# Output matmuls one batch behind instead of two, w_out loaded ahead of batch 1, packed-times-w_in in single two-bank PSUM tiles

## The chip, the cores and the metric

The kernel runs on one core of one Trainium2 chip. The metric is the device time of one execution in microseconds (us), median of several executions. An execution over 1.5% longer than the fastest of its kernel would count as slow.

## The reference

Eight batches of 576 tokens go through two attentions with 32 packed rows a head, then through a layer of width 2048 with `h * cos(h)`:

```python
p_packed = sm_attn(p, k, v)                 # 8 batches x 8 heads, 32 packed rows, head_dim 64
out = sm_attn(q, p_packed, p_packed)        # 576 queries a batch
x = out.transpose(0, 2, 1, 3).reshape(4608, 512)
h = x @ w_in                                # w_in 512 x 2048
g = h * cos(h)
return g @ w_out                            # w_out 2048 x 512, float32 out
```

## The kernel before

It never forms `x`. For each batch it computes PPW = packed rows times w_in (in the code `ppw`), and then the hidden layer as PPW times the normalised second-attention weights (`h_mm`, one call for each of 16 column blocks of 128, "layers" here). A batch goes through: key transpose, first scores and exp (`s1`), transposed probabilities (`a1T`), first product (`pp`), `ppw`, query transpose, second scores and exp (`s2`), sums and normalisation, 16 times `h_mm` with cos on ScalarE and the gate product on VectorE, and at last the output matmuls, 64 of 128x512 for an even batch and 80 for an odd one (`out_gen`). The order of instructions on each engine is the order of the program. The output matmuls are the "filler": `fill(n)` puts n of them between the steps of a later batch.

PSUM is the memory that matmuls write to. A tile in it comes free when ScalarE or VectorE has read it for the last time; reading it out to SBUF, the chip's other memory, is called evicting it. Here PSUM has a pool `A` of three tiles of two banks, for everything but the outputs and the `ppw` of batches 0 and 1, and a pool `O` of two tiles of one bank for these. One call of `ppw` is a "round".

```python
g_pool = ctx.enter_context(tc.tile_pool(name="g", bufs=3))          # gate products of a batch
A = ctx.enter_context(tc.tile_pool(name="psA", bufs=3, space=PSUM)) # [128, 2, 512] f32
O = ctx.enter_context(tc.tile_pool(name="psO", bufs=2, space=PSUM)) # [128, 512] f32

def ppw(b, n0, cnt, engs, pool=None):
    ...
    ps = [psa(), psa()]                      # two of the three tiles (one for each head parity y)
    for j in range(cnt):
        for x in range(4):
            for y in range(2):
                r = slice(64 * y, 64 * y + 64)
                nc.tensor.matmul(ps[y][32 * x:32 * x + 32, j, :], ppT[b % 2][r, 2 * x + y, :], ...)
    for y in range(2):                       # engs[0] evicts y = 0, engs[1] evicts y = 1
        ...

def h_mm(b, fc):
    ps = psa()
    ...                                      # 4 matmuls of 288 columns
    ACT.activation(out=csv, in_=ps[:, :, 0:HS], func=AF.Sin, bias=pihalf)
    def rest():                              # gate product: reads ps again, frees it
        V.tensor_tensor(out=gT..., in0=ps[:, :, 0:HS], in1=csv, op=ALU.mult)
        ...
    return rest

# batch 0 and batch 1: no filler; w_out is loaded while batch 1 is being prepared
...
set_filler(0)                                # output of batch 0 starts here, ahead of batch 2
fill(8); pp(2); fill(6); ppw(2, 0, 2, (V, ACT)); fill(4); ppw(2, 2, 2, (V, ACT)); fill(4)
for s in range(2, B):
    if s > 2:
        set_filler(s - 2)                    # two batches behind
    s2(s); fill(7); s1(s + 1); ...           # xbar q, xbar k, then a1_xbar: one DMA queue, in order
    fill(3); sums2(s, 0); fill(4); sums2(s, 1); normalise(s); fill(11)
    pieces = [(4, pp(s + 1)), (7, ppw(s + 1, 0, 2, ...)), (11, ppw(s + 1, 2, 2, ...))]
    for fc in range(NFC):                    # 16 layers; a piece where fc matches;
        rest = h_mm(s, fc)                   # the rest of the filler spread over the 16
        ...; rest(); fill(...)
for b in (B - 2, B - 1):                     # tail: 64 + 80 output matmuls
    set_filler(b)
fill(1000)
```

(Lines are cut and lambdas left out.)

The softmax here doesn't subtract the row's maximum and nothing guards it: scores larger than these inputs give would overflow.

## Time and profile before

| | before |
|---|---|
| time, median (range) | 306.99 us (306.8 to 307.25) |
| span of the profile | 303.9 us |
| TensorE busy | 257.9 us, 85% |
| ScalarE, VectorE busy | 190.8 us, 157.5 us |
| pure output matmuls at the end | 144, 31.2 us |

The rows for TensorE and its granted clock from the page's 40 slices (7.6 us each; busy share and clock in tenths):

```profile
PE   0766877978599678999998899999998999999993
PEclk9999796559869999999999999999999999999999
```

TensorE is loosely filled up to slice 16, and in most of slices 5 to 12 the clock is low too, so that the work it does takes longer. From slice 17 on it is nearly full.

The same by stage, from the windows view. Columns: window, its length, busy time (and instructions) of TensorE, weight loads, VectorE, ScalarE, GpSimd, then granted clock (the share of full speed that TensorE was given), DMA share, GB/s.

```profile
0.00:40.92 40.92, 25.62 (x218) 14.98 (x219) 22.00 (x45) 22.98 (x35) 10.11 (x18) 0.96 0.93 151
40.92:62.90 21.98, 15.54 (x203) 10.93 (x202) 11.10 (x21) 14.39 (x26) 9.38 (x10) 0.65 0.91 140
62.90:90.26 27.36, 22.70 (x158) 10.80 (x158) 16.52 (x24) 16.94 (x24) 7.67 (x7) 0.78 0.89 136
...
118.83:150.80 31.97, 30.35 (x237) 15.67 (x237) 18.38 (x27) 23.96 (x36) 6.38 (x7) 1.00 0.85 147
150.80:180.57 29.77, 26.52 (x221) 14.01 (x220) 17.73 (x26) 22.68 (x34) 6.38 (x7) 1.00 0.83 149
...
267.75:303.90 36.15, 31.24 (x145) 14.01 (x143) 4.12 (x6) 3.00 (x6) 0.61 (x1) 0.99 0.28 73
```

The windows are batch 0, the front of batch 1 (up to its first hidden matmul), its loop of layers with the front of batch 2, the stages of batches 3 and 4 (a "stage" runs from one `s2` to the next), and the tail. The last line is the price of the lag: 144 output matmuls alone, with VectorE and ScalarE idle. The second line is what is left unused: 22 us at a clock of 0.65.

A round of `ppw` in the stage of batch 4, from the timeline (start, length, engine, line, operation, count; in brackets the idle time before it and what ended it; lines of one kind together):

```profile
167.67 0.39 PE L183 MATMUL psA<-w_in_bf,ppT 64*32 64x512 bf16 x1
...
168.28 0.62 PE L183 MATMUL psA<-w_in_bf,ppT 64*32 64x512 bf16 x15 [0.23 <-DVE gT L234]
...
168.96 1.28 DVE L191 TENSOR_SCALAR PPW<-psA,r 128x1024 bf16<-128x1024 f32 x1 [0.73 <-PE psA L183]
168.99 1.11 ACT L189 ACTIVATE PPW<-psA,r 128x1024 bf16<-128x1024 f32 x1 [0.48 <-PE psA L183]
170.16 0.65 PE L227 MATMUL psA<-a2n,PPW 128*128 128x288 bf16 x4 [0.72 <-ACT PPW L189]
```

The round waits for a gate product to free its second tile, then the next layer waits for an eviction to free a tile: with two of three tiles in one round there is none left. Over the whole run, from the waits view (who waited for whom: us in total, times, longest):

```profile
PE psA L227 <- ACT PPW L189: 5.9, 10, 0.9
...
PE psA L160 <- POOL vp L77: 3.3, 1, 3.3
...
PE psA L183 <- DVE gT L234: 2.6, 9, 0.5
```

The line of VectorE in batch 0 on which the load order rests, from the timeline of that engine:

```profile
26.80 1.16 DVE L304 CAST p_bf<-p_raw 128x896 bf16<-128x896 f32 x2 [3.29 <-DMA p_raw<-in_p_dram]
```

The packed inputs of batches 1 to 7, loaded behind all of w_in, hold VectorE for 3.29 us, and with it the gate products of batch 0.

### The profile page before, as it was taken

Reading aid. Unit: us, or ns where it says so; the run is one execution under the profiler, and the core shown is the slowest. Engines: PE = TensorE matmul, PEld = TensorE weight load, DVE = VectorE, ACT = ScalarE, POOL = GpSimd, SP = SyncE. Lnnn points to the kernel's source line nnn. Section 1 sums busy time; section 2 is a strip of 40 time slices with the busy share of each in tenths; the row PEclk is TensorE's granted clock in tenths of the full one; section 3 lists DMA queues with packets and bytes.
Section 4 is the critical chain, followed back from the end, with each engine's and each line's share of the span. In section 5 each row is a group of like instructions: output and inputs, shape, how many; then the busy total and the mean of one; then the engine's idle time right before and its main releaser. Section 6 shows DMA issues by size and latency. Waiting matters only on the chain.

```text
span 303.9 us, 4986 instructions
## 1 busy us (share of the span) xinstructions
PE 257.9 (85%) x1996; PEld 136.8 (45%) x1996; DVE 157.5 (52%) x243; ACT 190.8 (63%) x285; POOL 55.8 (18%) x67
## 2 busy tenths in 40 slices
PE   0766877978599678999998899999998999999993
PEld 0633445535324433454445344544463455544441
DVE  2355884459342676466726672767277636630110
ACT  1366873789448578966796779666986786620000
POOL 8310028100540211230033003200400000000000
PEclk9999796559869999999999999999999999999999
DMA  7999409999199993989189929891740111222222
GB/s 110 205 213 212 72 3 152 194 203 168 31 168 201 179 190 76 175 150 218 42 157 169 200 56 176 166 162 36 140 95 10 40 55 37 69 61 79 69 69 69
DMA packets 62758, 37.08 MB, mean 122 GB/s; under 512 B 35488, under 2 KB 58016, under 8 KB 62736
## 3 DMA queue, kind: packets, MB, share of 16 engines
q0 software_dynamic: 23168, 18.81, 40.7%
q1 hardware_dynamic: 39568, 17.96, 27.9%
q8 instruction: 15, 0.25, 0.3%
q14 instruction: 7, 0.06, 0.1%
HBM read 37.22 MB, written 9.44 MB: 154 GB/s over the span
## 4 chain that ended last, share of the span: by engine, by line
PE 54%; ACT 17%; DVE 11%; DMA 10%; POOL 3%; issue 2%; SPq 0%; ACTq 0%; DVEq 0%; POOLq 0%
PE ot L262 28%; PE psA L227 15%; DMA p_raw<-in_p_dram 6%; DVE gT L234 6%; ACT cosT L231 5%; ACT PPW L189 4%; DMA a1T<-a 4%; PE psA L183 3%; DVE a2n L215 3%; PE psA L160 2%; ACT lns L207 2%; PE psA L124 2%; PE psA L102 2%; ACT lns L213 1%; ACT L381 1%
## 5 line engine op out<-in xcount | busy, mean ns | idle before, releaser
L262 PE MATMUL ot<-w_out_bf,gT 128*128 128x512 bf16 x512 | 130.9, 384 | 0.0
L231 ACT ACTIVATE cosT<-psA,pihalf 128x576 bf16<-128x576 f32 x128 | 93.3, 741 | 36.1 <-PE psA L227 34.4
L234 DVE TENSOR_TENSOR gT<-psA,cosT 128x576 bf16<-128x576 f32 x128 | 94.9, 755 | 37.6 <-ACT cosT L231 36.8
L227 PE MATMUL psA<-a2n,PPW 128*128 128x288 bf16 x512 | 88.5, 298 | 17.3 <-ACT PPW L189 5.9
L227 PEld LDWEIGHTS <-PPW 128*128 128x128 bf16 x512 | 50.9, 101 | 58.1 <-issue 24.7
L262 PEld LDWEIGHTS <-gT 128*128 128x128 bf16 x512 | 48.4, 99 | 47.9 <-issue 7.9
L238 POOL COPY joint<-gT 128x512 bf16<-128x512 bf16 x16 | 9.8, 611 | 149.5 <-DVE gT L234 149.5
L75 ACT COPY osb<-ot 128x512 f32<-128x512 f32 x18 | 10.5, 581 | 29.0 <-PE ot L262 28.9
L77 DVE COPY osb<-ot 128x512 f32<-128x512 f32 x18 | 12.3, 684 | 24.3 <-PE ot L262 24.3
L191 DVE TENSOR_SCALAR PPW<-psA,r 128x1024 bf16<-128x1024 f32 x12 | 15.4, 1284 | 9.9 <-PE psA L183 9.8
L77 POOL COPY vp<-vbf 96x3072 bf16<-96x3072 bf16 x7 | 19.2, 2749 | 4.0 <-DMA vbf<-in_v_dram 4.0
L215 DVE TENSOR_TENSOR a2n<-a2u,lns 128x576 bf16<-128x576 bf16 x16 | 11.4, 755 | 15.9 <-ACT lns L213 15.9
L189 ACT ACTIVATE PPW<-psA,r 128x1024 bf16<-128x1024 f32 x12 | 13.4, 1113 | 8.7 <-PE psA L183 8.7
L262 PE MATMUL ot<-w_out_bf,joint 128*128 128x512 bf16 x64 | 16.4, 379 | 0.0
L160 PE MATMUL psA<-a1T,vp 96*128 96x64 bf16 x192 | 8.7, 211 | 8.9 <-POOL vp L77 3.3
L170 ACT CAST ppT<-psA 64x128 bf16<-64x128 f32 x16 | 4.2, 260 | 17.4 <-DVE ppT L166 14.7
L183 PE MATMUL psA<-w_in_bf,ppT 64*32 64x512 bf16 x192 | 11.7, 400 | 2.7 <-DVE gT L234 2.6
L160 PEld LDWEIGHTS <-vp 96*128 96x128 bf16 x192 | 7.8, 110 | 10.8 <-POOL vp L77 5.4
L139 DVE RECIPROCAL r<-sums 128x2 f32<-128x2 f32 x8 | 1.3, 166 | 21.9 <-ACT a L133 21.9
L133 ACT ACTIVATE a<-psA 128x576 bf16<-128x576 f32 x16 | 10.2, 650 | 3.8 <-PE psA L124 3.8
L197 ACT ACTIVATE a2u<-psA,rs 128x576 bf16<-128x576 f32 x16 | 11.0, 736 | 2.4 <-PE psA L124 2.2
L166 DVE CAST ppT<-psA 64x128 bf16<-64x128 f32 x16 | 4.6, 289 | 12.9 <-PE psA L160 12.6
(54 smaller groups left out, 175.1 us busy)
## 6 DMA issues: line engine op xcount, KB each, us to landing
kbf<-in_k_dram POOLq DMA_DIRECT2D x8, 576.0 KB, 11.1
vbf<-in_v_dram POOLq DMA_DIRECT2D x8, 576.0 KB, 6.6
qbf<-in_q_dram POOLq DMA_DIRECT2D x8, 576.0 KB, 9.2
out_dram<-osb SPq DMA_DIRECT2D x24, 192.0 KB, 2.3
out_dram<-osb SPq DMA_DIRECT2D x24, 128.0 KB, 2.4
w_in_bf<-in_moe_w_in_dram POOLq DMA_DIRECT2D x4, 512.0 KB, 14.6
w_out_bf<-in_moe_w_out_dram POOLq DMA_DIRECT2D x4, 512.0 KB, 9.6
out_dram<-osb SPq DMA_DIRECT2D x24, 64.0 KB, 2.0
```

What stands on the lines that cost most here:

```text
L75: ACT.copy(out=out, in_=in_)
L77: eng.tensor_copy(out=out, in_=in_)
L160: nc.tensor.matmul(ps[:, 0, hp * 64:(hp + 1) * 64], vp[b][:, c, hp * 128:(hp + 1) * 128], a1T[b][0:TP, :, j, 32 * hp:32 * hp + 32], start= ...
L183: nc.tensor.matmul(ps[y][32 * x:32 * x + 32, j, :], ppT[b % 2][r, 2 * x + y, :], w_in_bf[r, x, (n0 + j) * 512:(n0 + j + 1) * 512], start=T ...
L189: ACT.activation(out=dst, in_=sv, func=AF.Copy, scale=r1[b][:, y:y + 1])
L191: V.tensor_scalar(out=dst, in0=sv, scalar1=r1[b][:, y:y + 1], scalar2=None, op0=ALU.mult)
L197: ACT.activation(out=a2u[b][:, y].rearrange("p (e x) -> p e x", e=2), in_=ps[y][:, :, 0:HS], func=AF.Exp, scale=rs1[b][:, y:y + 1])
L215: V.tensor_tensor(out=a2n[b][:, y], in0=a2u[b][:, y], in1=lns[b][:, y], op=ALU.mult)
L227: nc.tensor.matmul(ps[:, e, 0:HS], PPW[b][:, y, fc * 128:(fc + 1) * 128], a2n[b][:, y, e * HS:(e + 1) * HS], start=(y == 0), stop=(y == 1))
L231: ACT.activation(out=csv, in_=ps[:, :, 0:HS], func=AF.Sin, bias=pihalf)
L234: V.tensor_tensor(out=gT[b][:, fc, :].rearrange("p (e x) -> p e x", e=2), in0=ps[:, :, 0:HS], in1=csv, op=ALU.mult)
L262: nc.tensor.matmul(ps, w, w_out_bf[:, fc, :], start=(fc == 0), stop=(fc == NFC - 1))
```

## The change

Its intent: let the output matmuls of batch b run in the stage of batch b + 1. This frees one buffer of gate products, fills the idle TensorE of batch 1, and leaves 80 output matmuls for the tail instead of 144. w_out has to be there before batch 1. A round of `ppw` takes one PSUM tile instead of two, and half as many columns. The packed inputs move ahead of half of w_in, batch 1's value permute goes from GpSimd to VectorE, and batch 2's first product and `ppw` move into batch 1's loop.

```diff
-    g_pool = ctx.enter_context(tc.tile_pool(name="g", bufs=3))
+    g_pool = ctx.enter_context(tc.tile_pool(name="g", bufs=2))
...
-    def ppw(b, n0, cnt, engs, pool=None):
+    def ppw(b, n, engs, pool=A):
...
-            ps = [psa(), psa()]
+            t = psa()
+            ps = [t[:, 0, :], t[:, 1, :]]
...
     load("q", 0)
+    load_w_in(0)
+    load_w_in(1)
+    G.dma_start(out=p_raw[:, 2:, :], in_=p_rows[:, 2:, :])
+    load_w_in(2)
+    load_w_in(3)
     for n in range(4):
-        ... (w_in n)
-    G.dma_start(out=p_raw[:, 2:, :], in_=p_rows[:, 2:, :])
+        load_w_out(n)
+    load("k", 1); load("v", 1); load("q", 1); load("k", 2); load("v", 2); load("q", 2)
...
+    set_filler(0)
     pack_p(1, 8)
+    fill(4)
     pe_T("k", 1)
+    fill(3)
     s1(1)
+    permute_v(1, V)
+    fill(8)
     a1_pe(1)
-    permute_v(1)
+    fill(4)
     pp(1)
...                                # 43 output matmuls in the front of batch 1, 21 in its loop
+    def front(b, fc0):
+        return [(fc0, pp(b))] + [(fc0 + 3 + 2 * n, ppw(b, n, (V, ACT))) for n in range(4)]
+    slot(1, [(1, ppw(1, 2, ...)), (5, ppw(1, 3, ...))] + front(2, 6), [(8, begin_loads(3))])
 
     for s in range(2, B):
-        if s > 2:
-            set_filler(s - 2)
+        set_filler(s - 1)
...
-        pieces = [(4, pp(s + 1)), (7, ppw(s + 1, 0, 2, ...)), (11, ppw(s + 1, 2, 2, ...))]
+        slot(s, front(s + 1, 4) if nxt else [], [])
-    for b in (B - 2, B - 1):
-        set_filler(b)
+    set_filler(B - 1)
     fill(1000)
```

(Lambdas left out; `slot` is the old loop over the 16 layers, with the same spread of filler.)

More of the change, by code (lines that the diff above doesn't have):

```diff
@@ L175, in ppw @@
         if pool is O:
-            ps = [O.tile([128, 1, 512], FP32, name="ppw", tag="ot") for _ in range(2)]
+            ps = [O.tile([128, 512], FP32, name="ppw", tag="ot") for _ in range(2)]
         else:
-            ps = [psa(), psa()]
-        for j in range(cnt):
-            for x in range(4):
-                for y in range(2):
-                    r = slice(64 * y, 64 * y + 64)
-                    nc.tensor.matmul(ps[y][32 * x:32 * x + 32, j, :], ppT[b % 2][r, 2 * x + y, :],
-                                     w_in_bf[r, x, (n0 + j) * 512:(n0 + j + 1) * 512], start=True, stop=True)
+            t = psa()
+            ps = [t[:, 0, :], t[:, 1, :]]
+        for x in range(4):
+            for y in range(2):
+                r = slice(64 * y, 64 * y + 64)
+                nc.tensor.matmul(ps[y][32 * x:32 * x + 32, :], ppT[b % 2][r, 2 * x + y, :],
+                                 w_in_bf[r, x, n * 512:(n + 1) * 512], start=True, stop=True)
         for y in range(2):
-            dst = PPW[b][:, y, n0 * 512:(n0 + cnt) * 512].rearrange("p (j x) -> p j x", j=cnt)
-            sv = ps[y][:, 0:cnt, :]
+            dst = PPW[b][:, y, n * 512:(n + 1) * 512]
             if engs[y] is ACT:
-                ACT.activation(out=dst, in_=sv, func=AF.Copy, scale=r1[b][:, y:y + 1])
+                ACT.activation(out=dst, in_=ps[y], func=AF.Copy, scale=r1[b][:, y:y + 1])
             else:
-                V.tensor_scalar(out=dst, in0=sv, scalar1=r1[b][:, y:y + 1], scalar2=None, op0=ALU.mult)
+                V.tensor_scalar(out=dst, in0=ps[y], scalar1=r1[b][:, y:y + 1], scalar2=None, op0=ALU.mult)
     def s2(b):
@@ L283, in fill, with load_w_in, load_w_out, dup_p @@
             n -= 1
+    def load_w_in(n):
+        G.dma_start(out=w_in_bf[:, :, n * 512:(n + 1) * 512],
+                    in_=moe_w_in.rearrange("(a p) n -> p a n", p=128)[:, :, n * 512:(n + 1) * 512])
+    def load_w_out(n):
+        G.dma_start(out=w_out_bf[:, n * 4:(n + 1) * 4, :],
+                    in_=moe_w_out.rearrange("(a p) n -> p a n", p=128)[:, n * 4:(n + 1) * 4, :])
+    def dup_p(a, b):
+        for t in range(2):
+            V.tensor_copy(out=p_bf[:, a:b, t, :], in_=p_raw[:, a:b, :])
     nc.sync.dma_start(out=p_raw[:, 0:2, :], in_=p_rows[:, 0:2, :])
@@ L289 @@
     load("q", 0)
-    for n in range(4):
-        G.dma_start(out=w_in_bf[:, :, n * 512:(n + 1) * 512],
-                    in_=moe_w_in.rearrange("(a p) n -> p a n", p=128)[:, :, n * 512:(n + 1) * 512])
-    G.dma_start(out=p_raw[:, 2:, :], in_=p_rows[:, 2:, :])
+    load_w_in(0)
[3 more added lines that the diff above has]
+    load_w_in(3)
+    for n in range(4):
+        load_w_out(n)
+    load("k", 1)
+    load("v", 1)
+    load("q", 1)
+    load("k", 2)
+    load("v", 2)
+    load("q", 2)
     ACT.preload_act_table_set(EXP_SET)
@@ L300 @@
         V.memset(t[:, :, :, TP:128], 0.0)
-    def dup_p(a, b, eng):
-        for t in range(2):
-            eng.tensor_copy(out=p_bf[:, a:b, t, :], in_=p_raw[:, a:b, :])
-    dup_p(0, 2, V)
+    dup_p(0, 2)
     pack_p(0, 1)
@@ L309 @@
     s1(0)
-    load("k", 1)
+    permute_v(0, V)
     a1_pe(0)
-    permute_v(0, V)
     pp(0)
-    load("v", 1)
     pe_T("q", 0)
-    load("q", 1)
     s2(0)
-    ppw(0, 0, 1, (V, V), O)
+    ppw(0, 0, (V, V), O)
     sums2(0, 0)
     sums2(0, 1)
+    ppw(0, 1, (V, V), O)
     normalise(0)
-    dup_p(2, 16, V)
-    def load_w_out(n):
-        G.dma_start(out=w_out_bf[:, n * 4:(n + 1) * 4, :],
-                    in_=moe_w_out.rearrange("(a p) n -> p a n", p=128)[:, n * 4:(n + 1) * 4, :])
+    dup_p(2, 16)
     for n in range(4):
@@ L330 @@
             h_mm(0, fc)()
-            if fc == 4 * n + 1 and n < 3:
-                ppw(0, n + 1, 1, (V, ACT), O)
+            if fc == 4 * n + 1 and n in (1, 2):
+                ppw(0, n + 1, (V, ACT), O)
+    set_filler(0)
     pack_p(1, 8)
     ACT.preload_act_table_set(EXP_SET)
+    fill(4)
     pe_T("k", 1)
-    load("k", 2)
+    fill(3)
     s1(1)
+    permute_v(1, V)
+    fill(8)
     a1_pe(1)
-    permute_v(1)
+    fill(4)
     pp(1)
     pe_T("q", 1)
-    for n in range(4):
-        load_w_out(n)
@@ L344, with slot @@
-    load("v", 2)
-    load("q", 2)
+    fill(3)
+    ppw(1, 0, (V, ACT))
     s2(1)
-    ppw(1, 0, 1, (V, ACT), O)
+    fill(4)
     pe_T("k", 2)
+    ppw(1, 1, (V, ACT))
+    fill(3)
     s1(2)
-    ppw(1, 1, 1, (V, ACT), O)
-    a1_pe(2)
+    fill(4)
     sums2(1, 0)
+    fill(4)
     sums2(1, 1)
     normalise(1)
+    fill(6)
+    a1_pe(2)
     load("k", 3)
-    for fc in range(NFC):
-        h_mm(1, fc)()
-        if fc in (1, 5):
-            ppw(1, 2 + fc // 4, 1, (V, ACT), O)
+    def slot(s, pieces, hooks):
+        left = filler[1]
+        for fc in range(NFC):
+            rest = h_mm(s, fc)
+            while pieces and pieces[0][0] == fc:
+                pieces.pop(0)[1]()
+            rest()
+            while hooks and hooks[0][0] == fc:
+                hooks.pop(0)[1]()
+            done = left - filler[1]
+            fill((left * (fc + 1)) // NFC - done)
@@ L360, with begin_loads @@
+    def front(b, fc0):
+        return [(fc0, lambda: pp(b))] + [(fc0 + 3 + 2 * n, lambda n=n: ppw(b, n, (V, ACT))) for n in range(4)]
+    def begin_loads(b):
+        G.tensor_copy(out=gate, in_=xT["k", b][0:1, 0, 0:1])
+        for n, i in (("v", b), ("q", b), ("k", b + 1)):
+            load(n, i)
     permute_v(2)
     xbar("q", 2)
-    load("v", 3)
-    load("q", 3)
     xbar("k", 3)
-    load("k", 4)
-    set_filler(0)
-    ACT.preload_act_table_set(EXP_SET)
-    fill(8)
-    pp(2)
-    fill(6)
@@ L372 @@
-    ppw(2, 0, 2, (V, ACT))
-    fill(4)
-    ppw(2, 2, 2, (V, ACT))
-    fill(4)
+    slot(1, [(1, lambda: ppw(1, 2, (V, ACT))), (5, lambda: ppw(1, 3, (V, ACT)))] + front(2, 6),
+         [(8, lambda: begin_loads(3))])
     for s in range(2, B):
         nxt = s + 1 < B
-        if s > 2:
-            set_filler(s - 2)
-            ACT.preload_act_table_set(EXP_SET)
-            if nxt:
-                permute_v(s + 1)
-        else:
+        set_filler(s - 1)
+        ACT.preload_act_table_set(EXP_SET)
+        if nxt:
@@ L403 @@
                 load(n, b)
-        pieces = []
-        if nxt:
-            pieces = [(4, lambda: pp(s + 1)), (7, lambda: ppw(s + 1, 0, 2, (V, ACT))),
-                      (11, lambda: ppw(s + 1, 2, 2, (V, ACT)))]
-        left = filler[1]
-        for fc in range(NFC):
-            rest = h_mm(s, fc)
-            while pieces and pieces[0][0] == fc:
-                pieces.pop(0)[1]()
-            rest()
-            done = left - filler[1]
-            fill((left * (fc + 1)) // NFC - done)
-    for b in (B - 2, B - 1):
-        set_filler(b)
+        slot(s, front(s + 1, 4) if nxt else [], [])
+        fill(1000)
+    set_filler(B - 1)
     fill(1000)
```

## The prediction

> **What bounds the kernel now.** From 90 us on, TensorE. The windows view has it busy 26 to 28.5 us of each 29.5 to 30 us between 119 and 238 us. In the timeline the second-attention scores start at 90.3, 118.8, 150.8, 180.6, 212.1, 241.4 us; from 267 us on there is nothing but 148 output matmuls, 32.0 us, so 0.216 us each. Before 90 us nothing is saturated: TensorE is busy 14.8 of 21.2 us (41.7 to 62.9) at a granted clock of 0.64, 9.9 of 13.2 us (77.1 to 90.3). All output matmuls (576 x 0.216 = 124 us) start only at 77 us, because they run two batches behind and w_out is issued at 47.8 us.
>
> **What the change moves.**
> 1. Lag of one batch. Output matmuls per stage, before: 22 ahead of batch 2's stage, then 42, 80, 64, 80, 64, 80, and 144 after the last hidden layer. After: 64 during batch 1, then 80, 64, 80, 64, 80, 64, and 80 left. Tail: -64 x 0.216 = -13.8 us. Batch 1's front and loop get 42 more, into holes, and should keep the clock up (the Trainium skill, "TensorE: Matmul & The Clock Gate", part 1: throttled by default, activity releases it; the clock row agrees, 0.64 there against 1.00 later).
> 2. w_out before batch 1. The packed-input load lands at 26.8 us now and holds VectorE 3.3 us; ahead of half of w_in it should land near 20 us. Batch 0 then gains 2 to 3 us. The price: 2.1 MB at about 0.21 MB/us (DMA row) ahead of batch 1's keys delays those from 29 to about 39 us. Wanted at 39 to 41 us: just in time.
> 3. Batch 1's value permute on VectorE (0.95 us) in place of GpSimd (2.75 us): -1.5 us.
> 4. One PSUM tile per packed-times-w_in group. Now a round takes two of three tiles; the waits view shows 5.9 us of TensorE waiting for ScalarE's PPW evictions and 2.6 us for gT before those matmuls, about 1.5 us a round, 10 rounds or so. Afterwards: -1.5 to -2 us a stage. Evictions 4 x 0.68 instead of 2 x 1.28 us on VectorE: no loss.
>
> **Sum (span).** Batch 0 ends 39 instead of 42 us. Front of batch 1 about 22 us (47 output matmuls = 10 us hidden in it), its loop 19 us, limited by VectorE (16 x 0.77 + 6 x 0.67 + 2). Batch-2 stage starts at about 82 us, 8 earlier. Then 31 us for batch 2 (80 output matmuls; its transposed probabilities may come 1 to 2 us late, DMA is full there), 27.5 to 28 for 64-stages, 30.2 for 80-stages (now 29.4 to 29.8 and 31.5 to 32), last stage 23, tail 17.3 + 5. Together about 275; execution time is 3 us above the span: **278 us**, 8 in 10 between 270 and 288. Faster by over 2%: 0.96; within: 0.03; slower: 0.01.
>
> **What would show each step.** Tail of pure output matmuls about 17 us; clock between 40 and 62 us above 0.8; batch-1 keys landing near 39 us, TensorE's wait for them under 2 us; TensorE's wait for PPW evictions under 3 us; batch-2 scores starting near 82 us.
>
> **What would make it wrong.** Loads slower than 0.2 MB/us, so batch 1 waits; output matmuls delaying the front's latency chain, in order on TensorE; late loads for batch 3 (issue gated by the key transpose); VectorE becoming the limit in 64-stages, so they stay at 29 us.

## The result

The changed kernel takes 278.64 us (278.49 to 278.9, 4 runs), against 307.12 us before (306.8 to 307.42) in the same rounds. The ratio is 0.9074 (0.9058 to 0.909). A ratio here is the mean time of one kernel's fast runs over that of the other's of the same rounds, so not quite the ratio of the medians quoted. The experiments ran on other chips of the same kind, each beside the kernel before, whose median was 306.8 to 307.1 us there.

The two rows of the page after (slices of 6.9 us):

```profile
PE   0786889977879999998899999989999999999992
PEclk9999999999999999999999999999999999999997
```

The clock no longer falls. By stage, the windows view after (batch 0, front of batch 1, its loop, the stages of batches 2, 3, 4 and 5, the tail):

```profile
0.00:38.18 38.18, 24.91 (x218) 15.31 (x219) 22.91 (x46) 22.09 (x34) 12.57 (x21) 1.00 1.15 189
38.18:58.88 20.70, 18.92 (x246) 11.28 (x246) 11.23 (x22) 14.00 (x26) 6.99 (x7) 1.00 1.20 182
58.88:81.46 22.58, 17.74 (x158) 9.19 (x158) 16.43 (x26) 16.67 (x25) 2.98 (x5) 1.00 0.85 129
81.46:112.89 31.43, 29.82 (x237) 15.56 (x236) 18.40 (x29) 24.28 (x39) 6.38 (x7) 1.00 0.95 167
112.89:142.04 29.15, 26.74 (x221) 13.81 (x220) 17.55 (x28) 22.76 (x37) 6.38 (x7) 1.00 0.86 152
142.04:172.41 30.37, 29.61 (x237) 15.51 (x237) 18.69 (x30) 23.65 (x37) 6.38 (x7) 1.00 0.87 155
172.41:201.28 28.87, 26.73 (x221) 13.82 (x220) 17.79 (x28) 22.99 (x37) 5.62 (x6) 1.00 0.76 133
...
253.88:276.90 23.02, 18.08 (x85) 8.04 (x82) 3.50 (x5) 2.52 (x5) 0.61 (x1) 0.94 0.25 69
```

The span is 27.0 us shorter. Batch 2's stage starts at 81.46 instead of 90.26 us (8.8 us). The tail is 23.0 instead of 36.15 us; as the last window after begins with three output matmuls of the last stage (0.65 us), it shrank by 13.8 us. The rest, 4.4 us, came from the six stages between. The front of batch 1 has 43 output matmuls in it, where before it had none, and is 1.3 us shorter.

The waits of TensorE that answer to those shown before, one of ScalarE's, and VectorE's line in batch 0:

```profile
PE psA L160 <- DMA a1T<-a: 2.9, 3, 1.4
PE psA L226 <- ACT PPW L188: 2.1, 5, 0.5
...
PE psA L183 <- DVE gT L233: 0.2, 1, 0.2
```

```profile
ACT PPW L188 <- DVE PPW L190: 18.4, 28, 1.6
```

```profile
24.28 1.41 DVE L294 CAST p_bf<-p_raw 128x896 bf16<-128x896 f32 x2
```

These two waits of TensorE, for evictions and tiles, fell from 8.5 to 2.3 us together, and VectorE no longer waits for the packed inputs. A part only moved: scores, products and transposes now wait 2.1 us for ScalarE's evictions, so TensorE waits 4.2 us for them in all, where before the 5.9 us of the hidden layer were all. And there is a wait that was not there before: in all 28 rounds in pool `A` (four for each of batches 1 to 7), ScalarE's eviction starts only when VectorE's has ended. A round in the stage of batch 3, from the timeline, shows it:

```profile
132.50 0.41 PE L183 MATMUL psA<-w_in_bf,ppT 64*32 64x512 bf16 x8
...
133.21 0.74 DVE L190 TENSOR_SCALAR PPW<-psA,r 128x512 bf16<-128x512 f32 x1
133.50 0.65 PE L226 MATMUL psA<-a2n,PPW 128*128 128x288 bf16 x4
...
133.99 0.69 ACT L188 ACTIVATE PPW<-psA,r 128x512 bf16<-128x512 f32 x1 [0.57 <-DVE PPW L190]
...
134.57 0.58 ACT L75 COPY osb<-ot 128x512 f32<-128x512 f32 x1
...
135.04 1.39 ACT L230 ACTIVATE cosT<-psA,pihalf 128x576 bf16<-128x576 f32 x2
```

TensorE's matmuls of the round end at 132.91 us, ScalarE is free at 133.41 us, but it waits for VectorE until 133.99 us, and the next layer's cos stands behind that eviction (and behind the copy of an output tile) in ScalarE's order. Both halves are now one PSUM tile, and the program orders the two reads of one tile.

### The profile page after: what moved, and what is told of

The parts are those of the page before. It is cut to its first block, busy times and chain, and to the rows that moved or that the text cites. A ratio compares the mean times of both kernels' runs of the same rounds, so it can differ in the third digit from the quotient of the medians.

```text
span 276.9 us, 5007 instructions
## 1 busy us (share of the span) xinstructions
PE 244.3 (88%) x1996; PEld 130.9 (47%) x1996; DVE 158.3 (57%) x257; ACT 191.1 (69%) x296; POOL 53.2 (19%) x67
## 4 chain that ended last, share of the span: by engine, by line
PE 54%; ACT 18%; DVE 16%; DMA 6%; issue 4%; SPq 0%; ACTq 0%; POOLq 0%
PE ot L261 28%; PE psA L226 14%; DVE gT L233 6%; ACT cosT L230 5%; DVE PPW L190 5%; DMA a1T<-a 4%; ACT PPW L188 3%; DVE a2n L214 3%; PE psA L160 3%; PE psA L102 2%; DMA kbf<-in_k_dram 2%; PE psA L124 2%; ACT lns L206 2%; ACT lns L212 2%; PE psA L204 2%
## 5 line engine op out<-in xcount | busy, mean ns | idle before, releaser
L261 PE MATMUL ot<-w_out_bf,gT 128*128 128x512 bf16 x512 | 132.6, 380 | 0.0
L226 PE MATMUL psA<-a2n,PPW 128*128 128x288 bf16 x512 | 86.2, 291 | 10.8 <-DVE a2n L214 3.8
L261 PEld LDWEIGHTS <-gT 128*128 128x128 bf16 x512 | 46.7, 98 | 42.3 <-issue 6.9
L188 ACT ACTIVATE PPW<-psA,r 128x512 bf16<-128x512 f32 x28 | 19.2, 687 | 18.4 <-DVE PPW L190 18.4
L190 DVE TENSOR_SCALAR PPW<-psA,r 128x512 bf16<-128x512 f32 x28 | 20.8, 744 | 0.6 <-PE psA L183 0.5
L77 POOL COPY vp<-vbf 96x3072 bf16<-96x3072 bf16 x6 | 16.5, 2749 | 0.0
L160 PE MATMUL psA<-a1T,vp 96*128 96x64 bf16 x192 | 7.5, 199 | 4.5 <-DMA a1T<-a 2.9
L206 ACT ACTIVATE lns<-psA 128x576 f32<-128x576 f32 x16 | 10.4, 659 | 1.2 <-PE psA L204 0.7
L84 POOL DMA_DIRECT2D kbf<-in_k_dram x8 | 6.3, 787 | 21.6 <-PE psA L102 18.6
```

The source lines that it names most:

```text
L77: eng.tensor_copy(out=out, in_=in_)
L160: nc.tensor.matmul(ps[:, 0, hp * 64:(hp + 1) * 64], vp[b][:, c, hp * 128:(hp + 1) * 128], a1T[b][0:TP, :, j, 32 * hp:32 * hp + 32], start= ...
L188: ACT.activation(out=dst, in_=ps[y], func=AF.Copy, scale=r1[b][:, y:y + 1])
L190: V.tensor_scalar(out=dst, in0=ps[y], scalar1=r1[b][:, y:y + 1], scalar2=None, op0=ALU.mult)
L206: ACT.activation(out=lns[b][:, y].rearrange("p (e x) -> p e x", e=2), in_=ps[:, :, 0:HS], func=AF.Ln)
L226: nc.tensor.matmul(ps[:, e, 0:HS], PPW[b][:, y, fc * 128:(fc + 1) * 128], a2n[b][:, y, e * HS:(e + 1) * HS], start=(y == 0), stop=(y == 1))
```

## The experiments

All gave correct results.

### e1_lag2: only the lag undone

```diff
-    g_pool = ... bufs=2
+    g_pool = ... bufs=3
-    set_filler(0)                 # ahead of batch 1's front
-        set_filler(s - 1)
+        set_filler(s - 2)
-    set_filler(B - 1)
-    fill(1000)
+    for b in (B - 2, B - 1):
+        set_filler(b)
+    fill(1000)
```

> The changed kernel with only the lag undone: no output matmuls during batch 1, batches 2 to 7 take 64, 80, 64, 80, 64, 80 (432, as many as in the changed kernel), 144 in the tail. Theory (the 64 output matmuls put into batch 1 fall for the greater part into idle time of TensorE): the tail grows by 64 x 0.216 = 13.8 us, batch 1 gets 4 to 5 us shorter, total 287 to 289 us; granted clock in batch 1's front falls below 0.8. Rival A (all hidden): 292 us. Rival B (batch 1's stage is bound by TensorE, so the work only changes place): 279 to 281 us.

Measured: 294.01 us (292.16 to 294.72), ratio 0.9572 against 0.9074: the lag is worth 15.3 us (0.0498 x 307). The clock row of its page, and its windows for the front of batch 1 and for its loop:

```profile
PEclk9999995569759999999999999999999999999999
```

```profile
38.44:59.52 21.08, 15.62 (x202) 11.31 (x202) 10.58 (x21) 13.49 (x25) 6.99 (x7) 0.61 1.14 163
59.52:81.96 22.44, 16.05 (x138) 8.44 (x143) 15.84 (x24) 16.09 (x25) 2.97 (x5) 0.80 0.71 111
```

The theory's number fell and rival A came out, slightly exceeded. Without the 64 output matmuls the front and the loop take 43.5 us, with them 43.3 us: they cost nothing there. The clock tells why they fit so well. Without them it is 0.61 in the front, with them 1.00; the Trainium skill, "TensorE: Matmul & The Clock Gate", section "What's actually happening", says that the throttle is the default and that activity releases it, and these two windows show it on the same work. The filler pays for part of its own time by speeding up what it stands between. Above the 13.8 us of tail, the stages of batches 2 to 7 together took 1.8 us more in the profile with a lag of two (the slowest of its four executions; 81.96 to 256.78 us, against 81.46 to 254.53), with the same 432 output matmuls in another order. Most of this arose at a low clock again: from the scores of batch 2 to its first sums, with the same work in both kernels, it took 6.4 us (81.96 to 88.36) at a clock of 0.66 up to 90 us, against 4.8 us (81.46 to 86.24) at 1.00. Whether the order of the output matmuls matters besides is not shown.

### e2_pairs: only the old form of packed-times-w_in

```diff
-            t = psa()
-            ps = [t[:, 0, :], t[:, 1, :]]
+            ps = [psa(), psa()]
...
-    4 rounds of 512 columns, at layers fc0 + 3, + 5, + 7, + 9
+    2 rounds of 1024 columns, at layers fc0 + 3, + 7
```

> The changed kernel with only the old packed-times-w_in form (two PSUM tiles of the three, 1024 columns a round from batch 2 on). Theory as predicted (1.5 to 2 us a stage for 6 stages): 287 to 290 us. Rival, after reading the trace (the single tile gave most of it back, because ScalarE's eviction now waits for VectorE's eviction of the same tile, 18.4 us in 28 waits): only 281 to 284 us.

Measured: 286.86 us (286.12 to 288.84), ratio 0.9358: the single tile is worth 8.7 us (0.0284 x 307). That is at the theory's lower edge and well above the rival's 2.5 to 5.5 us, which fell. The edit changes two things at once, the tiles that a round takes and the size and number of rounds; e5 below changes the tiles alone. The waits view of this run:

```profile
PE psA L227 <- ACT PPW L189: 7.6, 14, 1.3
PE psA L183 <- DVE gT L234: 4.9, 11, 1.5
```

In these two lines TensorE waits 12.5 us, against 2.3 us in the changed kernel. In the profiled execution (288.84 us, the slowest of the four) batch 2's stage starts 3.2 us later (84.67 us). Batch 3's stage takes 31.5 instead of 29.15 us. But the clock was lower in both stretches, 0.93 in batch 1's loop and 0.95 in batch 3's stage, against 1.00. The stages of batches 2, 4, 5 and 6 take 0.4 to 1.5 us longer, so that the mean of the five is 1.4 us.

### e3_alt: one engine evicts a whole round

```diff
-    ppw(b, n, (V, ACT))
+    ppw(b, n, ((V, V), (ACT, ACT))[n % 2])     # from batch 1 on
```

> The changed kernel, but each packed-times-w_in group evicted by one engine alone (VectorE for even, ScalarE for odd groups), so the load of both engines stays the same and ScalarE never waits for VectorE's read of the tile. Theory (the serialised evictions delay the cos behind them): batch-1 loop 22.6 -> about 20 us, 64-stages 29.0 -> about 28 us, 272 to 276 us in all; ScalarE's wait for VectorE's PPW evictions (18.4 us) gone. Rival (TensorE and the throughput of VectorE set these stages, the waits are slack): 278 to 279 us.

Measured: 275.88 us (275.44 to 276.3), ratio 0.8987: 2.7 us better than the changed kernel, at the weak end of the theory, and the rival fell. ScalarE's 18.4 us of waits for VectorE's evictions are gone from the waits view. Batch 1's loop takes 21.9 us (not 20), the stage of batch 3 28.6 us (not 28). So the ordered evictions cost something, but less than their 18.4 us suggest: most of ScalarE's wait was slack. The run measures this wait alone. The two halves of a tile are still read one after the other, now by one engine, so the tile is held about as long; what that costs was not measured.

### e4_plate: packed inputs behind all of w_in

```diff
-    G.dma_start(out=p_raw[:, 2:, :], in_=p_rows[:, 2:, :])     # behind w_in part 1
     load_w_in(2)
     load_w_in(3)
+    G.dma_start(out=p_raw[:, 2:, :], in_=p_rows[:, 2:, :])
```

> The changed kernel with the packed inputs of batches 1 to 7 loaded after all of w_in again. Theory (VectorE waits for them with its queue in order): they land near 27 us instead of 21.6, batch 0 ends about 2.5 us later, total 280 to 281.5 us. Rival (batch 1's keys, landing near 39.5 us, gate the next stage anyway): under 0.7 us, 278.6 to 279.3 us.

Measured: 280.9 us (280.58 to 281.11), ratio 0.9153: 2.4 us worse. The theory stands: batch 2's stage starts 2.0 us later (83.44 us), and nothing behind it takes that up.

### e5_twotiles: one round in half of two tiles

```diff
-            t = psa()
-            ps = [t[:, 0, :], t[:, 1, :]]
+            ps = [psa()[:, 0, :], psa()[:, 0, :]]
```

> The changed kernel, but each packed-times-w_in group of 512 columns writes the first bank of two PSUM tiles instead of the two banks of one tile. Every round then takes two of the three tiles, as before the change, but twice as often as in the pair form. Theory (ScalarE waits for VectorE only because both read one tile; the tiles taken matter more than this wait): ScalarE's wait for VectorE's PPW eviction falls from 18.4 us to under 3 us, TensorE's waits for evictions and gT rise by 5 us or more, total 283 to 292 us. Rival (the serialised eviction is the larger evil): under 277 us.

Measured: 294.06 us (293.12 to 294.69), ratio 0.9583: 15.6 us worse, above the range that the theory gave. The timeline of a round, and TensorE's wait for tiles over the run:

```profile
136.67 0.75 DVE L189 TENSOR_SCALAR PPW<-psA,r 128x512 bf16<-128x512 f32 x1 [0.52 <-PE psA L182]
136.71 0.69 ACT L187 ACTIVATE PPW<-psA,r 128x512 bf16<-128x512 f32 x1 [0.26 <-PE psA L182]
```

```profile
PE psA L182 <- DVE gT L232: 8.9, 24, 1.5
```

The two evictions start 0.04 us apart again, so the order between them came from the one tile, as the theory said; ScalarE's wait for VectorE's evictions is gone. But each round of 512 columns now pays what a round of 1024 paid. The number of tiles taken outweighs the ordered evictions by far. Two tiles of one bank each, which would let the evictions run side by side without taking two of the three large tiles, were not tried.

### e6_before_single: only the new form of packed-times-w_in, in the kernel before

```diff
-    [(4, pp), (7, ppw(s + 1, 0, 2, ...)), (11, ppw(s + 1, 2, 2, ...))]
+    [(4, pp), (7, ppw(s + 1, 0, ...)), (9, ppw(s + 1, 1, ...)), (11, ppw(s + 1, 2, ...)), (13, ppw(s + 1, 3, ...))]
```

> The kernel before with only the new packed-times-w_in form (one tile of two banks, 512 columns, at layers 7, 9, 11, 13 in place of pairs at 7 and 11). Theory (worth 1.3 us a stage from batch 2 on, as undoing it in the changed kernel cost 8.2 us in all, 3.2 of it in batch 1's loop, which has no such groups here): 300 to 303 us. Rival (it pays only together with the shorter lag): 305.5 us or more.

Measured: 302.43 us (301.86 to 303.9), ratio 0.987 (0.9829 to 0.9912): 4.0 us faster, within the theory's range, and clear of noise though under 2%. The stages of batches 3 to 6 became 0.8 to 1.4 us shorter each, batch 2's 1.3 us longer. The form pays without the shorter lag too, but less than the 8.7 us that undoing it costs in the changed kernel. One likely reason is that there rounds stand in batch 1's loop as well.

### e7_wout_late: w_out behind batch 1's loads

```diff
-    for n in range(4):
-        load_w_out(n)
     load("k", 1); load("v", 1); load("q", 1)
+    for n in range(4):
+        load_w_out(n)
```

> The changed kernel with w_out loaded behind the keys, values and queries of batch 1 instead of ahead of them. Theory: batch 1's keys land near 29 us instead of 39, but the parts of w_out near 38, 40.5, 43 and 45.5 us, and TensorE, in order, waits for the last two in the 15 output matmuls ahead of the probability transposes: 1 to 3 us more, 279.6 to 281.6 us. Rival (all of it lands in time either way, order is worth nothing): 278 to 279.2 us.

Measured: 280.33 us (280.16 to 280.66), ratio 0.9139: 2.0 us worse (the intervals, 0.9117 to 0.9162 and 0.9058 to 0.909, do not touch). From the waits view:

```profile
PE ot L261 <- DMA w_out_bf<-in_moe_w_out_dram: 1.4, 1, 1.4
```

TensorE stood at one output matmul in front of the probability transposes, and batch 2's stage started 1.5 us later.

### e8_alt_rest: gate product ahead of the evictions

```diff
-            rest = h_mm(s, fc)
-            (pieces)
-            rest()
+            h_mm(s, fc)()
+            (pieces)                      # on top of e3_alt
```

> Evictions of a group by one engine, and in addition the gate product of a layer issued ahead of the group's evictions on VectorE. Theory (the tile of that layer comes free 1.5 us earlier where VectorE evicts, and TensorE waits for that tile two layers later): 64-stages from 28.5 to under 28 us, 273 to 275 us. Rival (VectorE then waits for the cos before it evicts, and the group's tile comes free later): 276 to 278 us.

Measured: 276.85 us (276.6 to 279.63), ratio 0.9045 (0.8997 to 0.9093): not better than e3_alt, so the theory fell. The stage of batch 3 took 29.1 us, not under 28. The waits view names the rival's mechanism:

```profile
PE psA L183 <- DVE PPW L190: 4.2, 9, 0.7
```

The next round waits for the tile of the last one, which VectorE now empties later.

### e9_vperm_pool: batch 1's value permute on GpSimd

```diff
-    load("v", 2); load("q", 2)            # at the start
-    permute_v(1, V)
+    permute_v(1)
     ...
     pe_T("q", 1)
+    load("v", 2); load("q", 2)
```

> The changed kernel with batch 1's value permute on GpSimd again (2.75 us instead of 0.95 on VectorE), and the value and query loads of batch 2 issued after it, as that queue's order requires. Theory as predicted: it lies on the chain to the first packed product, 1 to 1.5 us more, 279.6 to 280.2 us. Rival (the 8 output matmuls and the transposes between hide it, and VectorE is freed): 278.2 to 279.1 us.

Measured: 279.79 us (279.07 to 280.52), ratio 0.9127 (0.909 to 0.9164), 1.6 us above the changed kernel's and within the theory's range, but the intervals just touch. In the profiled execution (280.52 us, the slowest of the four) batch 2's stage starts 1.6 us later. Of this, 0.5 us were there before the copy: batch 1's packed transposes start at 38.72 instead of 38.18 us. The other 1.1 us stand in front of the first product:

```profile
43.99 2.75 POOL L77 COPY vp<-vbf 96x3072 bf16<-96x3072 bf16 x1
...
44.41 2.36 DVE L140 TENSOR_SCALAR rs<-r 128x2 f32<-128x2 f32 x1
...
46.69 0.54 DVE L77 COPY a1T<-psA 96x768 bf16<-96x768 bf16 x1
...
47.37 0.86 PE L160 MATMUL psA<-a1T,vp 96*128 96x64 bf16 x24 [1.12 <-DVE a1T L77]
```

The wait named is not the copy but VectorE's copy of the transposed probabilities behind it. VectorE stood at the small operation before it (L140), which took 2.36 us here, 0.17 us in the changed kernel, and ended with GpSimd's copy. The same operation also ended together with a GpSimd copy in the kernel before (1.27 us), and at batch 2's copy in the changed kernel (0.38 us). So, as far as the traces show, the copy delayed the first product through VectorE, by 1.1 us; the 0.5 us are not explained, and by the times alone the whole is not clear of noise.

### e10_alt_a1first: probabilities transposed ahead of the next queries and keys

```diff
+            a1_xbar(s + 1)
             xbar("q", s + 1)
             if s + 2 < B:
                 xbar("k", s + 2)
-            a1_xbar(s + 1)                # on top of e3_alt
```

> Evictions of a group by one engine (275.9 us by itself), and in addition the transpose of the probabilities issued ahead of the transposes of the next queries and keys, which it follows in the same queue. Theory (TensorE's wait for that transpose, 3.1 us in three stages, and the bubble after it go): 272.5 to 274.5 us, the wait under 0.5 us. Rival (the later query and key transposes push back loads or the next stage): 275.5 us or more.

Measured: 271.89 us (271.56 to 272.36), ratio 0.887: 6.3 us faster than the changed kernel (0.0204 x 307), and slightly better than the theory. It is the fastest version. The queue's transposes in batch 3's stage, first of the changed kernel:

```profile
115.58 3.11 SPq L93 DMA_TRANSPOSE qT<-qbf  x1
118.80 2.98 SPq L93 DMA_TRANSPOSE kT<-kbf  x1
121.87 1.66 SPq L144 DMA_TRANSPOSE a1T<-a  x1
```

and of this run:

```profile
114.74 1.46 SPq L144 DMA_TRANSPOSE a1T<-a  x1
116.31 3.38 SPq L93 DMA_TRANSPOSE qT<-qbf  x1
119.79 7.02 SPq L93 DMA_TRANSPOSE kT<-kbf  x1
```

The probabilities, which the same stage needs, stood behind 6 us of transposes that only the next stages need. TensorE's 3.1 us of waiting for them in e3_alt (2.9 us in the changed kernel) are gone from the waits view, and the stage of batch 3 takes 27.1 us (110.74 to 137.83), 2.1 us less than in the changed kernel. The key transpose takes 7.02 instead of 2.98 us now; the rival's fear that this would push back the next stage did not come true in the time.

## Why the prediction was right

The predicted time was 278 us (270 to 288), the measured one 278.64. The forecast was "faster", and it is. Its steps:

| step | predicted | measured |
|---|---|---|
| tail of pure output matmuls | about 17 us, then 5 | 18.1 us for 83, so 17.4 us for 80; then 4.9 us |
| worth of the lag | 13.8 us of tail, filler in holes | 15.3 us (e1) |
| clock in batch 1's front | above 0.8 | 1.00 (0.61 without filler, e1) |
| packed inputs first | 2 to 3 us | 2.4 us (e4) |
| batch 1's value permute | 1.5 us | 1.6 us by the times, not clear of noise; 1.1 us in the trace (e9) |
| TensorE's wait for PPW evictions | under 3 us | 2.1 us in the line that was 5.9 us; 4.2 us with the other matmuls that wait for them |
| single tile | 1.5 to 2 us a stage | 1.4 us on average over five stages, 8.7 us in all (e2); 0.8 to 1.4 us in the kernel before (e6) |
| batch 1's keys | near 39 us, no wait | issued at 19.3 us, landed at most 20.2 us later, so by 39.5; no wait shown |
| batch 2's stage starts | about 82 us | 81.46 us |
| batch 1's loop | 19 us | 22.6 us |
| stages with 64 output matmuls | 27.5 to 28 us | 29.15 and 28.9 us |
| stages with 80 | 30.2 us | 30.4 us |

Going from before to after in steps that were run: the single tile alone, ratio 0.987 (4.0 us); with it the new loads and the new order of batches 0 to 2 as well, 0.9572 (9.1 us more); with it the lag of one, 0.9074 (15.3 us more). (The middle one also has none of the 22 output matmuls ahead of batch 2.) Of the 9.1 us, e4 and e9 account for about 3.5 to 4, if they add up. The rest was not taken apart; the 3.3 us wait for a GpSimd copy at 79 us, which is gone, is a candidate.

The main mechanisms were right, and so was the range. That the total came within 1 us is luck: errors of 1 to 4 us cancelled.

Two terms of the sum were too small. Batch 1's loop took 3.6 us longer than predicted, each 64-stage 1 to 1.5 us. The prediction counted how long the evictions are ("no loss") and not their order: with one tile they run one after the other, and the cos of the next layer stands behind them. e3 shows 0.6 us of this in batch 3's stage and 0.7 us in the loop. The other part in the 64-stages was the wait for the transposed probabilities, which the prediction had only for batch 2: e10 takes 1.5 us more out of batch 3's stage and brings it to 27.1 us, below the predicted 27.5 to 28. What makes up most of the loop's 3.6 us is open. The prediction called the loop limited by VectorE, and warned that VectorE might keep the 64-stages at 29 us. They stayed at 29 us, but VectorE was busy 16.4 of 22.6 us in the loop and 17.6 of 29.15 us in batch 3's stage, so it was not the limit.

In the other direction batch 0 and batch 1's front were done at 58.9 us, where the prediction's terms give 61 us (39 and 22); with 19 us for the loop they give 80 us, and the text said 82; and the 3 us from span to time are 1.8 us. The span itself, 276.9 us, was under-estimated by 2 us.

Three figures of the text are slips: the front of batch 1 takes 43 output matmuls, not 47; of the 148 matmuls after 267 us four belong to the last stage; and 8.5 us of waits in 12 rounds are 0.7 us a round, not 1.5. Two rounds a stage make 1.4 us of it, which is what e2 measured.

## What to carry to other kernels

Work that depends on nothing near it, like output matmuls, belongs in the latency-bound prologue and not in the tail: in this kernel it cost nothing there, because it filled waits and also kept the clock at full speed for the work between. Before a step takes two of three buffers, see whether half the step in one buffer does; and then look whether two engines that read this buffer have become ordered. In a queue that runs in order, put first what the current stage needs, whatever was ready first.

## What the Trainium skill lacked or had wrong

- "PSUM — Partial Sum Buffer", section "PSUM bank collisions raise a hardware error", says that accesses to different banks run clean. The changed kernel's two evictions read different banks of one tile, and the program still ordered them: 28 waits, 18.4 us, none where the halves were two tiles (0.04 us apart in e5). The page lacks the remark that such a wait can come from the tile and not from the bank. No run here read two banks of one tile at once.
- "TensorE: Matmul & The Clock Gate", section "What's actually happening", describes how activity releases the throttle; it gives no figure for what useful filler is worth by this in a latency-bound stretch. Here: 64 more matmuls of 0.216 us, clock 0.61 to 1.00 in the front, and 43.3 us instead of 43.5 us for front and loop.
- "DMA: Bandwidth & Descriptors", section "DMA Transpose (X-bar)", has no remark that transposes issued on one queue should be ordered by need; here that order alone was worth 3.6 us (e10 against e3, by their ratios).
